# A chunked delta rule and a PReLU layer on one core: weight fetches issued one by one between the stages, and one step's squares moved

## The chip, the core and the metric

The kernel runs on one core of a Trainium2 chip. A core has four compute engines with instruction queues of their own: TensorE (PE, matrix products, with its weight loads shown as PEld), VectorE (DVE), ScalarE (ACT) and GpSimd (POOL). SyncE (SP) only issues DMAs here. The engines meet through semaphores. The metric is the device time of one execution in microseconds (us); lower is better.

## What is computed

Two blocks follow each other. The first is a delta-rule attention with batch 4, 8 heads, 768 tokens and head size 48; the second is a feed-forward layer on the 3072 tokens of width 384, with 2048 hidden units and a PReLU with one slope per unit.

```python
for t in range(S):
    y[:, :, t] = q[:, :, t] @ state
    v_old = state.T @ kt                     # kt: the key of t, divided by its norm
    state = state + beta_t * outer(kt, v[:, :, t] - v_old)
x = y as (tokens, heads * head size)         # 3072 x 384
h = x @ w_in                                 # 384 x 2048
g = max(h, 0) + alpha * min(h, 0)
out = g @ w_out                              # 2048 x 384
```

All is float32.

## The kernel before

**Tiling.** The 768 tokens are cut into 12 chunks of 64. A *step* is one chunk of two batch rows, so there are 24 steps, numbered from 0. A step needs its keys, values and queries, the squares of its keys (for the norms), the products of its keys with each other, the inverse of a triangular matrix made from these, a product with the carried state, its outputs, and the next state. Two steps of one chunk give 256 rows for the feed-forward layer. The first layer (`ffn_in`, products on L1068) has 16 column blocks of 128, each the sum of three products; after two column blocks, a relu on ScalarE (L1078) and two slope operations on VectorE (L1080) empty the PSUM bank. Two banks (`p_ffn`) take turns. The second layer of the first two chunks is `ffn_out` (L1111).

**Weights.** Both weight matrices are loaded once and rounded into another form on the chip. `w_in` is loaded in 12 pieces of 512 KB (piece 1 to 12; three pieces serve four column blocks), `w_out` in 16 pieces of 384 KB. A piece is fetched by one DMA from SP into a staging space (L216) and then converted by two ScalarE operations (L233, L235), one of VectorE (L249) and one of POOL or VectorE (L256). The staging spaces are borrowed: pieces 1 to 6 of `w_in` land where `w_out` will be, the others in `space_out`, `more`, `sums` and `turned`; the pieces of `w_out` use three slots of `space_out` and free parts of `w_out`. A fetch call `fetch(n)` issues all pieces up to the n-th that have not been issued. The converting generator also issues fetches when a piece is done: for `w_in` all the rest after the first piece (argument `limit` 0, L1654), for `w_out` one further piece per converted piece, if its staging space is free.

**Order.** The order of the instructions on each engine is the order in which the program's Python emits them; nothing reorders them. The engines then run their queues in order, each instruction waiting for its semaphores. SP too issues its DMAs in order: a DMA that waits holds all that are queued behind it. DMAs from SP use eight completion semaphores in turn, so a DMA also waits until the one eight places ahead has landed.

**The stages around the change.** After a prologue, `first_chunk` (from L1572) finishes steps 0 and 1; within it the q loads of steps 2 and 3 are issued (L1604), with `fetch_in(11)` behind them (L1605). `second_pair` (from L1763) does steps 2 and 3 and mixes in the first layer of chunk 0: the calls `alongside(p, c)` emit p matmuls of that layer and c conversion half-steps. `keys(k)` in it flips the keys of step k, squares them on ScalarE (L379), sums the squares on VectorE (L386) and issues the load of the keys three steps later. `fetch_out(4)` stands in it at L1813. A `weave` follows in which the first layer of chunk 1 (`ffn_in(1)`) runs beside the rest of the `w_out` conversion, beside `statics` (from L1620: squares, norms and key products of steps 8 and on) and beside `eliminate`, the triangular inverse on VectorE (L558, L564). `squares(n)` is the ScalarE square and the VectorE sum for step n; `weigh(n)` takes the root (L401, L402) and the reciprocal.

Of the kernel before, what the change touches and what calls it, by code (L numbers as in the profile page):

```python
# [43 lines left out]
def kernel(  # L44
# [105 lines left out]
    def load_q(n):  # L150
        if n < N:
            fetch(q, n, q_pad[n % NQ][:, :, 0:D])
# [36 lines left out]
    def weights(pieces, stages, ids, done, limit=None, pool=0, pace=None):  # L189

        count = len(pieces)
        fetched, begun = [], []  # L200

        def words(i):
            w = stages[ids[i]]
            dst, src = pieces[i]
            shape = list(dst.shape)
            n = shape[1] * (shape[2] if len(shape) > 2 else 1)
            w = w[:, 0 : 2 * n]
            if len(shape) > 2:
                return w.rearrange("p (f e) -> p f e", f=shape[1]), n
            return w, n  # L210

        def fetch(n):
            while len(fetched) < min(n, count):
                i = len(fetched)
                assert ids[i] not in ids[len(done) : i]
                nc.sync.dma_start(out=words(i)[0], in_=pieces[i][1].bitcast(U32))  # L216
                fetched.append(i)

        def flat(x):
            return x.rearrange("p f d -> p (f d)") if len(x.shape) > 2 else x  # L220

        def halves(i):
            w = flat(words(i)[0]).rearrange("p (e w) -> p e w", w=2)
            return w[:, :, 0], w[:, :, 1], flat(pieces[i][0])

        def begin_half(n):

            while len(begun) < min(n, 2 * count):
                i = len(begun) // 2
                assert i < len(fetched)  # L230
                lo, hi, dst = halves(i)
                if len(begun) % 2 == 0:
                    nc.scalar.activation(dst.bitcast(U32), lo, ACT.Copy, scale=2.0**-29)  # L233
                else:
                    nc.scalar.activation(  # L235
                        lo.bitcast(FP32), hi.bitcast(FP32), ACT.Prelu,
                        scale=2.0**-112, alpha=-(2.0**32),
                    )
                begun.append(i)

        def begin(n=None):
            begin_half(len(begun) + 1 if n is None else 2 * n)

        def finish():
            for i in range(count):
                n = 2 * min(i + 2, ahead[0])
                begin_half(max(n - 1, 2 * (i + 1)))
                lo, _, dst = halves(i)
                nc.vector.tensor_scalar(  # L249
                    out=lo, in0=lo, scalar1=3, scalar2=None, op0=ALU.logical_shift_left  # L250
                )
                yield

                begin_half(n)
                engine = nc.gpsimd if i < pool else nc.vector
                engine.tensor_tensor(  # L256
                    out=dst.bitcast(U32), in0=lo, in1=dst.bitcast(U32), op=ALU.add
                )
                done.append(i)
                n = len(fetched)  # L260
                last = min(count, limit or count, n + pace if pace else count)
                while n < last and ids[n] not in ids[i + 1 : n]:
                    n += 1
                    fetch(n)
                yield

        return fetch, begin, finish()
# [240 lines left out]
    NJ = 4  # L508
# [912 lines left out]
    in_done, out_done = [], []  # L1421
# [150 lines left out]
    def first_chunk(convert, mask):  # L1572

        both = (0, 1)
        ahead[0] = 0
        for n in both:
            place_small(n)

        def own(n):
            return own_values(n, ps_big()[:, :, 0:WY])  # L1580

        def rounds(i):
            for x in [one_round(n, i, ps_big()[:, :, 0:WY]) for n in both]:
                now(x)

        now(matrix(0, ps_big()[:, :, 0 : G * C]))
        turn_matrix(0, nc.scalar)
        scale_first(1, nc.vector)
        z_0 = own(0)
        now(z_0)  # L1590
        turn_values(0, nc.gpsimd)
        convert(1)
        now(matrix(1, ps_big()[:, :, 0 : G * C]))
        z_1 = own(1)
        now(z_1)
        turn_values(1, nc.scalar)
        turn_matrix(1, nc.scalar)
        convert(2)
        begin_in(4)
        for n in both:  # L1600
            mask(n)
        nc.gpsimd.memset(q_pad[0][0:1, 0, 0:1], 0.0)
        for i in both:
            load_q(i + 2)  # L1604
        fetch_in(11)  # L1605
        for i in range(3):
            rounds(i)
        y_0 = outputs(0, ps_big()[:, :, 0:WY])
        now(y_0)
        convert(2)  # L1610
        now(outputs(1, ps_big()[:, :, 0:WY]))
        to_ffn(0, ps_ffn())
        to_ffn(1, ps_ffn())
        convert(1)
        for n in range(2, NJ):
            place_small(n)
        begin_in()
        ahead[0] = FT * DM

    def statics(first, last):  # L1620
        if first > 0:
            squares(first)
        for n in range(first, last + 1):
            if n < last:
                squares(n + 1)
            now(weigh(n))
            flips(n, N)
            yield
            if n > 0:
                load_early(n + NKE)  # L1630
            if n > first:
                now(grams(n - 1))
            yield
        now(grams(last))
        yield
# [15 lines left out]
    stages += [sums.rearrange("p i s e -> p (i s e)").bitcast(U32)[:, 2 * n : 3 * n]]  # L1651
    stages += [rest.bitcast(U32)]
    ids = [*range(len(pieces))]
    fetch_in, begin_in, conv_in = weights(pieces, stages, ids, in_done, 0, len(pieces))  # L1654
    PARTS_IN = 2 * len(pieces)

    pieces = [(w_out[:, f], moe_w_out[f * 128 : (f + 1) * 128]) for f in range(FT)]
# [101 lines left out]
    def alongside(products, pieces, *gens):  # L1759
        gens = [(part(first_in, products), products), (part(convert_on, pieces), pieces), *gens]  # L1760
        weave(*[x for x in gens if x[1] > 0])

    def second_pair():  # L1763

        n, m, x = 2, 3, NJ
        both = (n, m)

        def burst(step, width):
            p = ps_big()
            pieces = []  # L1770
            for i in range(2):
                pieces += step(n + i, p[:, :, i * width : (i + 1) * width])
            now(pieces)

        def keys(k):
            flip_more(k)
            squared(k)
            norms(k)
            load_early(k + NKE)

        def through(i, p):
            now(through_state(i, None, p))

        now(next_state(0))
        load_late(2)
        for i in both:
            scale_first(i)
        alongside(2, 2)
        now(next_state(1))
        load_late(3)  # L1790
        keys(x)
        alongside(3, 3)
        burst(matrix, G * C)
        for i in both:
            turn_matrix(i, nc.gpsimd)
        now(weigh(x))
        alongside(3, 2)
        for i in both:
            flips(N, i)
            load_q(i + 2)  # L1800
        alongside(2, 1)
        keys(x + 1)
        alongside(2, 1)
        y = ps_big()
        through(n, y[:, :, 0 : G * D])
        alongside(2, 1)
        through(m, y[:, :, G * D : 2 * G * D])
        now(weigh(x + 1))
        alongside(3, 2)
        burst(own_values, G * D)  # L1810
        for i in both:
            turn_values(i, nc.gpsimd)
        fetch_out(4)  # L1813
        alongside(3, 2)
        now(grams(x))
        alongside(2, 2)
        burst(lambda i, p: one_round(i, 0, p), G * D)
        load_v(4)
        alongside(2, 1)
        keys(x + 2)  # L1820
        alongside(2, 2)
        burst(lambda i, p: one_round(i, 1, p), G * D)
        now(weigh(x + 2))
        alongside(2, 1)
        now(grams(x + 1))
        alongside(2, 1)
        burst(lambda i, p: one_round(i, 2, p), G * D)
        alongside(2, 1)
        keys(x + 3)
        alongside(2, 1)  # L1830
        now(grams(x + 2))
        now(weigh(x + 3))
        alongside(2, 1)
        burst(outputs, G * D)
        alongside(3, 2)
        now(grams(x + 3))
        alongside(2, 1)
        for i in both:
            to_ffn(i)
        alongside(2, 1, (part(blocks, 5), 5))  # L1840
        for i in both:
            now(next_state(i))
            load_late(i + 2)
            load_v(i + 3)
            alongside(2, 0, (part(blocks, 1), 1))
        alongside(IN_PARTS - 45, 0, (part(blocks, 1), 1))
# [174 lines left out]
```

## Time and profile before

| | us |
|---|---|
| median of 3 runs (656.79 to 661.25) | 657.06 |
| the profiled execution | 656.12 |
| its span, from first to last instruction | 654.3 |
| PE busy / VectorE / ScalarE / POOL | 634.4 / 481.5 / 258.4 / 122.5 |

The profile is of one execution, and all durations below come from it; 1.8 us lie outside its span. "L1068" is line 1068 of the kernel before. A row of the timeline is: start, duration, engine, line, operation, output <- inputs, and in brackets how long the engine stood idle before it and what ended that. "Granted clock" is the share of full speed that the throttle lets TensorE have; "DMA share" is the mean busy share of the 16 DMA engines, and can exceed 1 a little in short stretches.

### The profile page before, as it was taken

Reading aid. Unit: us, or ns where it says so; the run is one execution under the profiler, and the core shown is the slowest. Engines: PE = TensorE matmul, PEld = TensorE weight load, DVE = VectorE, ACT = ScalarE, POOL = GpSimd, SP = SyncE. Lnnn points to the kernel's source line nnn. Section 1 sums busy time; section 2 is a strip of 40 time slices with the busy share of each in tenths; the row PEclk is TensorE's granted clock in tenths of the full one; section 3 lists DMA queues with packets and bytes.
Section 4 is the critical chain, followed back from the end, with each engine's and each line's share of the span. In section 5 each row is a group of like instructions: output and inputs, shape, how many; then the busy total and the mean of one; then the engine's idle time right before and its main releaser. Section 6 shows DMA issues by size and latency. Waiting matters only on the chain.

```text
span 654.3 us, 21366 instructions
## 1 busy us (share of the span) xinstructions
PE 634.4 (97%) x9157; PEld 560.6 (86%) x9157; DVE 481.5 (74%) x1155; ACT 258.4 (39%) x605; POOL 122.5 (19%) x243
## 2 busy tenths in 40 slices
PE   6979999999999999999999999999999999999997
PEld 4657878566789988989988988988989999999997
DVE  5846789768999788578769658769868668477383
ACT  6637655245445244144244143133145145042140
POOL 6257511010001000010000010000044043062250
PEclk9979999999999999999999999999999999999999
DMA  8876454112422222121121111121121210100000
GB/s 159 231 205 167 144 115 134 36 39 50 76 44 45 42 47 38 37 51 38 35 43 26 30 41 32 28 45 29 33 43 27 50 27 2 35 5 2 24 1 25
DMA packets 108974, 37.27 MB, mean 57 GB/s; under 512 B 102048, under 2 KB 105264, under 8 KB 108880
## 3 DMA queue, kind: packets, MB, share of 16 engines
q1 hardware_dynamic: 107008, 35.42, 24.7%
q8 instruction: 72, 1.18, 0.7%
q10 hardware_dynamic: 1872, 0.49, 0.4%
q14 instruction: 22, 0.18, 0.1%
HBM read 31.17 MB, written 4.72 MB: 55 GB/s over the span
## 4 chain that ended last, share of the span: by engine, by line
PE 86%; DVE 6%; ACT 3%; issue 2%; DMA 2%; SPq 1%; POOL 0%; ACTq 0%
PE p_ffn L1068 23%; PE p_ffn L1133 17%; PE p_more L1385 8%; PE p_more L1301 5%; PE p_ffn L1111 4%; PE p_ffn L1291 3%; PE p_ffn L1385 3%; PE p_ffn L1296 2%; PE p_pair L423 2%; PE p_pair L800 2%; PE p_pair L923 2%; PE p_pair L740 2%; PE p_pair L910 2%; PE p_pair L479 2%; PE p_pair L788 1%
## 5 line engine op out<-in xcount | busy, mean ns | idle before, releaser
L1068 PE MATMUL p_ffn<-xt,w_in 128*128 128x256 f32 x768 | 178.6, 385 | 1.9 <-DVE sums L1080 1.2
L1068 PEld LDWEIGHTS p_ffn<-xt,w_in 128*128 128x128 f32 x768 | 142.2, 191 | 22.7 <-issue 2.0
L1078 ACT ACTIVATE act<-p_ffn 128x512 f32<-128x512 f32 x56 | 33.4, 597 | 82.2 <-PE p_ffn L1068 82.0
L1080 DVE SCALAR_TENSOR_TENSOR act<-act,al_t,p_ffn 128x256 f32<-128x256 f32 x112 | 48.6, 476 | 22.8 <-ACT act L1078 22.6
L1325 POOL TENSOR_TENSOR k_t<-k_t 128x128 f32<-128x128 f32 (+1 forms) x48 | 29.5, 615 | 167.5 <-ACT k_t L1320 165.0
L564 DVE TENSOR_TENSOR block<-block,prod 128x30 f32<-128x30 f32 (+9 forms) x150 | 49.9, 333 | 5.1
L558 DVE TENSOR_TENSOR prod<-block 128x30 f32<-128x30 f32 (+9 forms) x150 | 49.2, 328 | 3.6 <-POOL block L548 2.3
L412 POOL TENSOR_TENSOR beta_t<-beta_t,rec 128x8 f32<-128x8 f32 x20 | 5.2, 258 | 237.3 <-DVE rec L406 227.7
L1133 PE MATMUL p_ffn<-w_out,act 128*128 128x192 f32 x288 | 49.6, 328 | 0.0
L966 ACT COPY xt<-p_pair 128x384 f32<-128x384 f32 x22 | 10.4, 479 | 93.1 <-PE p_pair L962 79.3
L1133 PEld LDWEIGHTS p_ffn<-w_out,act 128*128 128x128 f32 x288 | 46.6, 190 | 0.3
L1325 POOL TENSOR_TENSOR block<-block 128x128 f32<-128x128 f32 (+1 forms) x48 | 27.6, 575 | 16.7 <-ACT block L1320 14.2
L1291 PE MATMUL p_ffn<-xt,w_in 128*128 128x256 f32 x96 | 28.7, 381 | 0.5 <-DVE o_sb L1153 0.5
L752 ACT COPY inv<-p_pair 32x256 f32<-32x256 f32 x40 | 14.5, 362 | 24.9 <-DVE u L914 24.1
L1339 DVE SCALAR_TENSOR_TENSOR act<-block,al_t,act 128x256 f32<-128x256 f32 x32 | 19.7, 657 | 5.2 <-ACT block L1335 5.1
L1153 DVE TENSOR_TENSOR o_sb<-u,p_ffn 128x192 f32<-128x192 f32 x24 | 8.0, 352 | 20.8 <-PE p_ffn L1133 20.0
L923 PEld LDWEIGHTS p_pair<-u,a_t 64*64 64x64 f32 x768 | 13.9, 137 | 10.5 <-issue 8.4
L792 ACT COPY y<-p_pair 128x384 f32<-128x384 f32 x22 | 10.6, 481 | 30.8 <-PE p_pair L788 29.2
L818 DVE TENSOR_TENSOR r<-v_raw,p_pair 64x192 f32<-64x192 f32 (+1 forms) x60 | 21.2, 353 | 1.0
L1385 PE MATMUL p_more<-w_out,act 128*128 128x192 f32 x128 | 21.9, 329 | 0.0
L1320 ACT COPY k_t<-p_more 128x512 f32<-128x512 f32 x16 | 9.4, 586 | 31.4 <-PE p_more L1301 26.7
L800 PE MATMUL p_pair<-beside,k_t 48*64 48x112 f32 x704 | 21.4, 259 | 0.2 <-ACT beside L451 0.2
(280 smaller groups left out, 1412.8 us busy)
## 6 DMA issues: line engine op xcount, KB each, us to landing
v_raw<-in_v_dram SPq DMA_DIRECT2D x48, 96.0 KB, 2.9
qp<-in_q_dram SPq DMA_DIRECT2D x48, 96.0 KB, 3.0
out_dram<-o_sb SPq DMA_DIRECT2D x90, 48.0 KB, 1.6
kl<-in_k_dram SPq DMA_DIRECT2D x88, 48.0 KB, 2.5
space_out<-in_moe_w_out_dram SPq DMA_DIRECT2D x11, 384.0 KB, 4.0
ke<-in_k_dram SPq DMA_DIRECT2D x43, 96.0 KB, 3.0
w_out<-in_moe_w_in_dram SPq DMA_DIRECT2D x6, 512.0 KB, 7.2
w_out<-in_moe_w_out_dram SPq DMA_DIRECT2D x5, 384.0 KB, 4.7
```

Of the source, the lines that this page charges most:

```text
L558: nc.vector.tensor_tensor(out=prod, in0=r[:, 0:j, j : j + 1].to_broadcast([128, j, n]), in1=r[:, j : j + 1, j + 1 : HB].to_broadcast([128, ...
L564: nc.vector.tensor_tensor(out=r[:, 0:j, j + 1 : HB], in0=r[:, 0:j, j + 1 : HB], in1=prod, op=ALU.add)
L800: nc.tensor.matmul(p[half(t ^ a), a, g], k_t[n][dims(a), g, half(t)], beside[bp][dims(a), t, g])
L923: nc.tensor.matmul(p[half(t), a, g], a_t[n][half(t ^ a), a * G + g], us[n][half(t ^ a), a, g])
L1068: nc.tensor.matmul(p_h[:, i], w_in[:, t, (f + i) * 128 : (f + i + 1) * 128], xt[:, t], start=(t == 0), stop=(t == KT - 1),)
L1078: nc.scalar.activation(g, p_h, ACT.Relu, scale=-1.0)
L1080: nc.vector.scalar_tensor_tensor(out=g[:, i], in0=g[:, i], scalar=al_t[:, f + i : f + i + 1], in1=p_h[:, i], op0=ALU.mult, op1=ALU.add,)
L1133: nc.tensor.matmul(p, x(i), w(i), start=(i == 0), stop=(i == FP - 1))
L1291: nc.tensor.matmul(p[:, f * 256 : f * 256 + 256], w(2, f), xt[:, 2], start=True, stop=False)
L1301: nc.tensor.matmul(q[:, j], a, b, start=True, stop=True)
L1325: nc.gpsimd.tensor_tensor(out=dst, in0=a, in1=b, op=ALU.add)
L1385: nc.tensor.matmul(p, x(i), w(i), start=(i == 0), stop=(i == FP - 1))
```

## The change

Three edits. First, the conversion of `w_in` no longer issues the remaining fetches when its first piece is done (`limit` 6 in place of 0), and `fetch_in(11)`, which stood behind the q loads, becomes `fetch_in(8)`; pieces 9 to 12 are issued one at a time in `second_pair`. Second, `fetch_out(4)` becomes four calls, of which the last three stand behind the v load of step 4 and behind two of the `keys`. Third, the squares of step 8 are emitted at the end of `second_pair`, behind `to_ffn`, and no longer at the start of `statics`.

```diff
@@ first_chunk
         for i in both:
             load_q(i + 2)
-        fetch_in(11)
+        fetch_in(8)
@@ statics
-        if first > 0:
+        if first > 2 * NJ:
             squares(first)
@@ the pieces of w_in
-    fetch_in, begin_in, conv_in = weights(pieces, stages, ids, in_done, 0, len(pieces))
+    fetch_in, begin_in, conv_in = weights(pieces, stages, ids, in_done, 6, len(pieces))
@@ second_pair
         now(next_state(0))
         load_late(2)
+        fetch_in(9)
...
         now(next_state(1))
         load_late(3)
+        fetch_in(10)
         keys(x)
...
         for i in both:
             flips(N, i)
             load_q(i + 2)
+        fetch_in(11)
         alongside(2, 1)
         keys(x + 1)
+        fetch_in(12)
...
             turn_values(i, nc.gpsimd)
-        fetch_out(4)
+        fetch_out(1)
...
         load_v(4)
+        fetch_out(2)
         alongside(2, 1)
         keys(x + 2)
+        fetch_out(3)
...
         keys(x + 3)
+        fetch_out(4)
...
         for i in both:
             to_ffn(i)
+        squares(x + 4)
         alongside(2, 1, (part(blocks, 5), 5))
```

On SP this gives the order: q loads, pieces 7 and 8, four k_late loads, piece 9, four k_late loads, piece 10, a k and four q loads, piece 11, a k load, piece 12, the first piece of `w_out`, a v load, the second, a k load, the third to fifth, a k load, the sixth to eighth, and behind eight k_late and four v loads the ninth and tenth.

## The prediction

> **What bounds the kernel now.** I read the page first (busy time, slices, queues), then the waits of TensorE (PE), then the chain of work that ended last, in order of time. From the page:
>
> ```profile
> PE 634.4 (97%) x9157; PEld 560.6 (86%) x9157; DVE 481.5 (74%) x1155; ACT 258.4 (39%) x605; POOL 122.5 (19%) x243
> ...
> PEclk9979999999999999999999999999999999999999
> ...
> q8 instruction: 72, 1.18, 0.7%
> ```
>
> PE is busy for 97% of the span, so time can be won only where PE stands idle or runs slowly: the third slice (33 to 49 us) is the one dip of the granted clock after the start. The waits of PE (total us, times, longest) beyond the first input loads:
>
> ```profile
> PE p_pair L923 <- issue: 4.3, 1, 4.3
> PE p_ffn L1068 <- DVE sums L1080: 1.2, 1, 1.2
> PE p_pair L850 <- issue: 1.1, 1, 1.1
> ```
>
> Two of the three are "issue": nothing that the profile shows was awaited. The chain (start, us, what) around the larger one, and two stretches (busy time of PE, PEld, DVE, ACT, POOL, then granted clock, DMA share, GB/s):
>
> ```profile
> 35.20 0.28 PE p_pair L923 x3
> 35.48 4.28 issue
> 39.76 1.10 PE p_pair L923 x29
> 40.86 1.56 PE p_ffn L962 x6
> 42.42 1.04 PE p_pair L939 x32
> 43.46 1.55 PE p_ffn L1068 x4
> 45.01 0.61 PE p_pair L939 x32
> ```
> ```profile
> 35.00:40.00 5.00, 0.52 (x11) 0.43 (x15) 0.64 (x2) 0.48 (x1) 4.28 (x8) 0.76 0.99 365
> 40.00:45.00 5.00, 5.00 (x75) 3.75 (x73) 2.65 (x5) 2.19 (x4) 0.74 (x2) 0.56 0.89 134
> ```
>
> PE stops in the middle of a group of 32 equal matmuls while the DMA engines are at 0.99; then it works at about half clock until 45 us. What does it await? The instruction queue moved 1.18 MB in 72 packets, 16 KB each, and 2 x 9157 PE instructions over 72 packets is 254 to a packet, or 127 matmuls with their weight loads. PE had done 600 matmuls when it stopped at 35.48, and 509 more when it stopped at 63.78 us: 4.0 packets. So I take both pauses for PE out of instructions, its next packet standing behind weights: six pieces of 512 KB are issued from 29.1 to 33.9 us, four of 384 KB from 55.9 to 58.7 us. Counting 127 matmuls back, the late packets could be asked for at 31.7 and 59.0 us, so they took 8.1 and 5.9 us; the packet begun at 31.7 had come within 3.0 us of 28.7, before the pieces moved (102 to 154 GB/s there).
>
> [...]
>
> **a. The first pause.** SyncE (SP) issues its DMAs in order. Before, the six late w_in pieces (7 to 12) went out ahead of four q loads; after, the q loads go at 34.12 us (as before, held by POOL's memset at 33.99) and take 0.65 us each, and only pieces 7 and 8 follow, near 36.8. Between 31.7 and 35.3 us no weights are in flight, so the packet should be there: 4.28 us go. With the pause goes the slow clock. The chain from 39.76 to 45.01 is 5.25 us; at full clock the same work is 0.49 (29 of L923, from 64 in 1.08 at 76.55), 0.82 (six L962, at 80.65), 0.62 (L939) and 1.06 us (four L1068), 2.99 in all, and 0.25 appears: the second three transposes wait for VectorE's copy of y (0.56), covered only by the first three (0.41), plus a hop. Saved 2.0, in all **-6.3 us**. Bounds: -6.6 (nothing appears) and -5.0 (1.3 us of pause left). From 45 to 63 us the chain is PE without a gap, so the gain is passed on.
>
> [...]
>
> What is late next? Each piece must land before ScalarE (ACT) converts it, for ACT is in order. With SP at 0.65 us per small load and 0.45 per piece, and ACT's rows (48.46, 54.36, 57.76, 60.69, 61.99) earlier by 6.3, pieces 7, 9, 10, 11 and 12 are issued near 36.8, 40.9, 44.0, 48.3 and 50.0 and wanted at 42.2, 48.1, 51.5, 54.4 and 55.7: 5.4 to 7.5 us each. Weight DMAs landed in 3.0 to 11.0 us, median 5.4, the longest being the last of six in a row; alone I take 4. Cost 0; a late piece 12 falls into ACT's idle 2.96 us before 66.34, and PE wants pieces 10 to 12 only at 77.56.
>
> **b. The second pause.** At the old 55.9 to 58.7 four w_out pieces went out; now one goes, then the v load, then a second. The packet wanted at 64.9 is asked for with about two pieces ahead instead of four: **-1.1 us**, bounds -0.3 and -1.15.
>
> **c. Later w_out pieces, and the squares.** Old times. (The fourth fetch call finds four pieces fetched already; fetching stays one piece behind.) *Piece 3* now stands behind the k load that waits until 67.86, is issued at 69.2, not 57.8, and is wanted by ACT at 70.08. Landing in 3.6 us, as piece 10 did (92.03 to 95.63), it holds ACT for 2.7 us; relu (71.46) and its slopes on VectorE slip, and the u sums end near 75.7, not 73.9. PE wants them at 76.48: nothing lost, 0.8 us left. *Piece 6* goes at 76.65 behind the next k load and is wanted at 78.15, but ACT's next work waits for PE until 81.17: free up to a landing of 4.0. *Piece 9* is different. It was issued near 77.5; now it comes behind eight k_late and four v loads, where piece 10 was, at 92.03. The old rows of ACT there:
>
> ```profile
> 93.16 0.55 ACT L233 ACTIVATE w_out<-space_out 128x384 uint32<-128x384 uint32 x1
> 93.62 0.57 ACT L1078 ACTIVATE sums<-p_ffn 128x512 f32<-128x512 f32 x1
> ...
> 95.63 0.56 ACT L233 ACTIVATE w_out<-space_out 128x384 uint32<-128x384 uint32 x1 [0.98 <-DMA space_out<-in_moe_w_out_dram]
> ```
>
> The first becomes piece 9, landing at 95.6; the relu behind it frees a PSUM bank for PE's group at 96.34. Step by step: 95.6 + 0.46 (convert) + 0.60 (relu) + 0.87 (two slopes) + 0.14 = 97.7, so that group starts 1.35 us later than before.
>
> The squares of step 8 leave this stretch: ACT's square (0.47) and VectorE's sum (0.5) run near 82 us, where they push the slopes back by 0.4. In return ACT's L401 at 90.31 no longer waits for a sum made at 89.73, the relu of 91.59 can run two us sooner, and PE's wait of 1.15 us at 92.09 shrinks to about 0.15. But the next group waits for piece 9 anyway, so this gain is lost inside the 1.35. Together **+1.3 us**; bounds -0.2 (landing in 3.0, and SP 0.9 us sooner: one k_late load took 1.51 us there, not 0.60) and +2.0 (VectorE, 98% busy from 100 to 110, stays behind and delays one more group).
>
> **Sum.** -6.3 - 1.1 + 1.3 = -6.1 on the profiled execution's 656.12 us: 650.0. The median of the runs shown, 657.06, lies 0.94 above that execution, so **650.9**; own range 649.1 (-6.6 - 1.15 - 0.2) to 653.8 (-5.0 - 0.3 + 2.0), both with the 0.94. One per cent, about what a measurement can tell from no change here, is 6.6 us: the forecast sits just inside it.
>
> **Rivals.**
> *A, the pauses are no fetch* (0.08). Then 4.28, 2.0 and 1.1 stay and only c acts: 656.12 + 1.3 + 0.94 = 658.4. For it: the profile names no releaser. Against: the counts, and DMA at 0.99 beside the one pause, full at 61 to 63 us before the other.
> *B, slower: late w_out pieces in ACT's order* (0.05). If pieces 3, 6 and 9 land in L us instead of 3.6, PE loses (L - 4.4) + (L - 4.0) + (L - 2.3), against 7.4 won: it turns slower at L = 6.0. At 9.1, as the piece into sums took, it loses 16.6: 666.3. For it: six of the moved pieces took 6 to 11 us. Against: those stood in one burst; w_out pieces took 4.0 and 4.7 us (medians), and between 65 and 69 us the DMA engines are all but idle.
> *C, the packets are late elsewhere* (0.13). From 34 to 53 us loads and pieces now follow each other closely, and a packet wanted near 52 or 57 us may wait. [...]
>
> **Chances.** The forecast 0.74, A 0.08, B 0.05, C 0.13. The range 649.0 to 655.0 takes in the forecast's bounds and C, and leaves out A, B and 0.05 of tails. Faster by over 1% (below 650.5) is nearly half of the forecast's share and a tail of it where c costs nothing: 0.40. Slower by over 1% is B from L = 8.2 on: 0.04. Within 1%: 0.56.
>
> **What would show it.** Right: no "issue" wait of over 0.5 us on PE, granted clock 1.00 from 35 to 45 us, L939's second group at 45.01 now near 38.7; ACT waiting for a DMA at its third and ninth w_out piece; PE waiting for DVE L1080 once, for about 2 us, at the old 95 to 98, and no more at 92. Wrong: pauses that stay in place (A), or turn up at another multiple of 127 matmuls (C); ACT waits of over 5 us for DMAs before 82 (B).

## The result and the profile after

The changed kernel takes 653.44 us (median of 20 runs, 652.05 to 657.0) against 656.91 us of the kernel before (20 runs, 654.94 to 661.25): a ratio of 0.9946, 95% interval 0.9932 to 0.9961. It is faster by half a per cent, 3.5 us. The forecast was 650.9; the measured time lies inside the range, on the same side, and the gain is a little over half of what was expected. The profiled execution after took 652.51 us with a span of 650.7 us, 3.6 us less than the span before.

From the page after (busy time per engine; the granted clock in 40 slices):

```profile
PE 633.7 (97%) x9157; PEld 559.3 (86%) x9157; DVE 481.9 (74%) x1155; ACT 257.9 (40%) x605; POOL 124.0 (19%) x243
...
PEclk9999999999999999999999999999999999999999
```

The dip of the clock in the third slice is gone, and the work of the engines is what it was. The chain of work that ended last, around the place of the old pause (start, us, what):

```profile
34.41 0.28 PE p_pair L923 x3
34.69 0.44 issue
35.13 0.70 PE p_pair L923 x29
35.83 0.02 issue
35.85 0.57 DVE y L866
...
38.71 0.61 PE p_pair L939 x32
```

The pause has shrunk from 4.28 to 0.44 us, the 29 matmuls of L923 behind it take 0.70 us in place of 1.10, and the wait of the transposes for VectorE's copy of y (L866) has appeared, as the working said. The same stretches as before in the kernel after (busy time of PE, PEld, DVE, ACT, POOL, then granted clock, DMA share, GB/s), with five microseconds ahead of them:

```profile
30.00:35.00 5.00, 4.27 (x195) 3.66 (x195) 4.16 (x8) 3.85 (x8) 4.96 (x5) 1.00 0.02 5
35.00:40.00 5.00, 4.68 (x109) 3.68 (x110) 4.18 (x7) 2.27 (x5) 4.41 (x6) 1.00 0.69 129
40.00:45.00 5.00, 5.00 (x87) 4.26 (x86) 2.85 (x6) 4.94 (x11) 4.26 (x7) 1.00 1.05 293
```

The DMA engines stand idle (0.02) while the packet of instructions that PE wants at 34.7 us can be fetched, and the granted clock stays at 1.00. What was lost again shows in the waits of PE in the kernel after (total us, times, longest), of which these are the ones near the change:

```profile
PE p_ffn L1068 <- DVE prod L558: 2.4, 1, 2.4
PE p_pair L923 <- DVE u L905: 1.4, 2, 1.2
PE p_pair L850 <- issue: 0.7, 1, 0.7
...
PE p_ffn L1068 <- DVE sums L1080: 0.5, 1, 0.5
PE p_pair L923 <- issue: 0.4, 1, 0.4
```

and in ScalarE's timeline (start, duration, engine, line, operation, in brackets the idle time before it and what ended that):

```profile
56.35 0.69 ACT L233 ACTIVATE w_in<-sums 128x512 uint32<-128x512 uint32 x1 [1.88 <-DMA sums<-in_moe_w_in_dram]
59.65 0.68 ACT L233 ACTIVATE w_in<-turned 128x512 uint32<-128x512 uint32 x1 [1.89 <-DMA turned<-in_moe_w_in_dram]
...
68.10 0.57 ACT L233 ACTIVATE w_out<-space_out 128x384 uint32<-128x384 uint32 x1 [3.35 <-DMA space_out<-in_moe_w_out_dram]
...
77.30 0.56 ACT L233 ACTIVATE w_out<-w_out 128x384 uint32<-128x384 uint32 x1 [3.41 <-DMA w_out<-in_moe_w_out_dram]
...
90.45 0.55 ACT L233 ACTIVATE w_out<-space_out 128x384 uint32<-128x384 uint32 x1 [4.90 <-DMA space_out<-in_moe_w_out_dram]
```

ScalarE waits for pieces 11 and 12 of `w_in` and for pieces 3, 6 and 9 of `w_out`; before, it waited for one piece in all, 0.98 us. Of the signs that the prediction named, three came: the clock, the second group of L939 near 38.7 us, and the waits for pieces 3 and 9. Three went another way: an "issue" wait of 0.71 us is left, piece 6 is awaited too, and PE's one wait of about 2 us (2.38) stands at 86.2 us, two groups of products ahead of where it was forecast. The further "issue" waits of rival C have not come: PE has only those of 0.7 and 0.4 us. Laying the same PE instruction of both profiles side by side shows where PE's lead was won and lost:

| PE instruction | before | after | lead |
|---|---|---|---|
| second group of L923, start | 35.20 | 34.41 | 0.79 |
| L423 behind the second L939 | 45.55 | 39.26 | 6.29 |
| L850 behind the second pause | 64.93 | 58.18 | 6.75 |
| L923 of steps 2 and 3 | 76.48 | 71.04 | 5.44 |
| third group of `ffn_in(1)`'s later half, behind L423 | 96.34 | 92.54 | 3.80 |
| first L1111 | 112.25 | 108.52 | 3.73 |

The first 0.79 us come from ahead of that group. 0.51 of them are a short stop that the kernel before makes at 31.9 us (more of it below) and the kernel after does not; the rest lies in the prologue, where PE's waits for the key loads add up to 5.2 us before and 4.6 after (4.4 to 5.4 in the profiles of this case). In the profiles below, the second group of L923 starts between 34.4 and 37.1 us in kernels that are the same up to there. For the rest I therefore use the stretch from that group to the first L1111: 77.05 us before, 74.11 after. The short stop lies outside it.

### The profile page after: what moved, and what is told of

The parts are those of the page before. It is cut to its first block, busy times and chain, and to the rows that moved or that the text cites. A ratio compares the mean times of both kernels' runs of the same rounds, so it can differ in the third digit from the quotient of the medians.

```text
span 650.7 us, 21360 instructions
## 1 busy us (share of the span) xinstructions
PE 633.7 (97%) x9157; PEld 559.3 (86%) x9157; DVE 481.9 (74%) x1155; ACT 257.9 (40%) x605; POOL 124.0 (19%) x243
## 4 chain that ended last, share of the span: by engine, by line
PE 81%; DVE 6%; DMA 3%; SPq 2%; ACT 2%; issue 1%; POOL 0%; ACTq 0%
PE p_ffn L1068 21%; PE p_ffn L1133 17%; PE p_more L1385 8%; PE p_more L1301 5%; PE p_ffn L1111 4%; PE p_ffn L1291 3%; PE p_ffn L1385 3%; PE p_ffn L1296 2%; PE p_pair L423 2%; PE p_pair L800 2%; PE p_pair L923 2%; PE p_pair L740 2%; PE p_pair L910 2%; PE p_pair L939 1%; DMA space_out<-in_moe_w_out_dram 1%; PE p_pair L479 1%
## 5 line engine op out<-in xcount | busy, mean ns | idle before, releaser
L966 ACT COPY xt<-p_pair 128x384 f32<-128x384 f32 x22 | 10.4, 478 | 90.7 <-PE p_pair L962 76.9
L1111 PE MATMUL p_ffn<-w_out,act 128*128 128x384 f32 x64 | 21.7, 490 | 0.0
```

The source lines that it names most:

```text
L1111: nc.tensor.matmul(p_o[u], gs[f // 2][:, f % 2, u * 128 : (u + 1) * 128], w_out[:, f], start=(f == 0), stop=(f == FT - 1),)
```

## The experiments

Theory T is the prediction's: the first pause is PE out of instructions behind a burst of weights, and what is lost later comes from late `w_out` pieces. Rival W puts that loss on the late pieces 11 and 12 of `w_in`; rival S on the moved squares; rival A says the pauses are no instruction fetch.

**Is the pause an instruction fetch?** The kernel before, with 32 more small matmuls in the prologue:

```diff
-    short(5, ps_one())
+    short(37, ps_one())
```

> The kernel before with 32 more matmuls of 32x32 in the prologue (about 0.7 us of PE), their result unused. If the first pause is PE out of instructions at a packet's border, PE stops 32 matmuls earlier in the program: not behind the third of the 32 matmuls of the second group of L923, but with some 3 left in the group of 32 before it (the first L923, its last three), again after about 600 recorded matmuls from the start, and for 3 to 5 us. The second pause moves 32 matmuls earlier too. If the pause belongs to an instruction or to a hidden wait at that place of the program (rival A), it stays behind the third matmul of the second group, now after about 632.

Its PE timeline, and PE's counts (the x behind the second number) up to the two pauses:

```profile
32.07 0.32 PE L850 MATMUL p_pair<-act 64*64 64x48 f32 x4 [0.34 <-DVE act L888]
35.40 2.49 PE L850 MATMUL p_pair<-act 64*64 64x48 f32 x92 [3.02 <-issue]
37.67 1.34 PE L850 MATMUL p_pair<-r,act 64*64 64x48 f32 x36
40.50 0.99 PE L850 MATMUL p_pair<-r,act 64*64 64x48 f32 x26 [1.49 <-issue]
```
```profile
0.00:35.30 35.30, 26.72 (x473) 20.06 (x473) 22.53 (x74) 21.89 (x56) 15.96 (x54) 1.00 0.88 219
...
0.00:39.50 39.50, 30.34 (x601) 23.49 (x601) 24.75 (x78) 22.04 (x56) 17.80 (x56) 0.96 0.90 234
```

PE stops after 473 and after 601 records. In the kernel before it had stood after 473 (0.51 us, put down to ScalarE's L235) and after 600 (4.28 us):

```profile
32.42 0.61 PE L850 MATMUL p_pair<-act 64*64 64x48 f32 x26 [0.51 <-ACT w_out L235]
```
```profile
0.00:31.70 31.70, 24.74 (x473) 17.81 (x473) 23.08 (x76) 20.32 (x54) 14.09 (x53) 1.00 0.85 190
...
0.00:36.00 36.00, 27.61 (x600) 20.21 (x600) 25.80 (x80) 22.70 (x57) 18.03 (x57) 1.00 0.86 202
```

The places in the program have moved by 64 records: the first stop came 68 records into the run of L850 on `act`, now 4; the second three records into the second group of L923, now in the L850 ahead. So the 32 added matmuls stand in the trace as 64 records, two for each; my "32 earlier" left that out. The counts stay and the instructions differ: the stop belongs to a border in the instruction stream, not to an instruction. The two stops together cost 4.8 us in the one and 4.5 in the other; which of the two borders is hit harder differs. The expected 3 to 5 us did not come at the second border (1.49), and the second pause of the kernel before, expected 32 matmuls earlier, did not come at all. This is one execution.

The kept traces hold more: the start and length of each packet of the instruction queue. They settle it.

| stop of PE, and where | packet moves, us | PE goes on | behind the packet's end |
|---|---|---|---|
| before, 473 records | 29.75 to 30.81 | 32.42 | 1.61 |
| before, 600 | 37.44 to 38.33 | 39.76 | 1.43 |
| before, second pause | 62.70 to 63.68 | 64.93 | 1.25 |
| shifted, 473 | 33.02 to 33.98 | 35.40 | 1.42 |
| shifted, 601 | 37.91 to 38.86 | 40.50 | 1.64 |
| after, 600 | 32.78 to 33.80 | 35.13 | 1.33 |
| after, second pause | 55.26 to 56.71 | 58.18 | 1.47 |

After every stop PE goes on 1.25 to 1.64 us behind the end of a packet. The packet behind the large pause began to move 5.0 us after PE had passed the border ahead (32.42 us), with the DMA engines at a share of 0.92 in between; in the kernel after, with the DMA engines idle (0.06), 1.1 us after it (31.63 us). Once begun, it took 0.9 and 1.0 us. So PE waits for its instructions, and the packet stands behind the weights before it moves: rival A falls.

**Which edit wins, which loses?** `w_in` spread alone (the `w_out` edits and the squares undone), and `w_in` spread with the squares moved:

```diff
-        fetch_out(1)
+        fetch_out(4)
...
-        fetch_out(2)
...
-        fetch_out(3)
...
-        fetch_out(4)
```

> Only the w_in fetches are spread; the w_out fetch call of four pieces and the squares are as before. Theory T (the first pause and its slow clock are worth 6.3 us, and what is lost later comes from the late w_out pieces 3, 6 and 9): 6.3 us faster than before, near 650.6; no wait of PE for VectorE's u at the outputs of steps 2 and 3, PE's wait of about 1.15 us for the slopes near the old 92 us stays, no ACT wait of over 1.5 us for a w_out piece. Rival W (the loss comes from pieces 11 and 12 of w_in, which hold ACT for 1.9 us twice, and this runs on): PE still waits 1.2 us for u, and the gain is 3.5 to 5 us only.

> The changed kernel with the w_out fetch call of four pieces put back: w_in spread and squares moved. Theory T: 6.3 plus about 1.0 for the squares, 7.3 us faster than before, near 649.6, and 3 to 4 us faster than the changed kernel. Rival W: no faster than the changed kernel, 3.5 to 4.5 us ahead of before.

The spread alone takes 651.74 us against 656.64 of before: 0.9914 (0.9882 to 0.9945); with the squares 650.83: 0.9891 (0.9844 to 0.9938). The first gain, 4.9 us, lies in W's range (3.5 to 5) as well as near T's 6.3; what tells them apart is PE's wait for u. Both kernels were timed again, beside the changed kernel.

> The changed kernel once more, as the measure for the three beside it: 3 to 4 us faster than before, with the waits of its first profile (PE for u about 1.2 us, one of about 2.4 us for the slopes after the transposes).

> w_in spread and squares moved, w_out fetched four at once, timed again beside the changed kernel. Theory T (late w_out pieces 3, 6 and 9 cost the changed kernel about 3 us, less the 0.5 of the second pause): 2 to 3.5 us faster than the changed kernel, no PE wait over 0.6 us between 40 and 105 us. Rival W (late pieces 11 and 12 of w_in): within 1 us of the changed kernel.

> w_in spread alone, again. If the squares are worth what PE's wait at the old 92 us shows (1.15 us, less 0.5 that is left in the kernel with both): 0.6 to 1.2 us slower than with the squares moved. If they are worth nothing (rival S): the same within 0.3 us, or faster.

| kernel | median, us | ratio to before | 95% interval | L923 to L1111, us |
|---|---|---|---|---|
| before | 657.01 | 1 | | 77.05 |
| as changed | 654.55 | 0.9965 | 0.9945 to 0.9985 | 74.11 and 74.40 |
| `w_in` spread alone | 650.85 | 0.9908 | 0.9889 to 0.9927 | 71.38 and 71.27 |
| `w_in` spread, squares moved | 650.80 | 0.9902 | 0.9885 to 0.9919 | 70.02 and 70.62 |

The intervals of the last two do not meet that of the changed kernel: without the spread of `w_out` the kernel is some 3.7 us faster (654.55 - 650.80), and faster than both kernels of this change. The changed kernel gained 2.5 us here, where 3 to 4 were expected, with the expected waits. Rival W falls as the sole cause: with `w_in` spread alone, ScalarE waits for pieces 11 and 12 as it does in the changed kernel, and PE does not wait for u (VectorE's L905, from which the outputs of steps 2 and 3 are made). ScalarE's waits for DMAs in that kernel, and PE's only wait of over 0.5 us from 40 to 105 us:

```profile
56.22 0.68 ACT L233 ACTIVATE w_in<-sums 128x512 uint32<-128x512 uint32 x1 [1.21 <-DMA sums<-in_moe_w_in_dram]
60.02 0.67 ACT L233 ACTIVATE w_in<-turned 128x512 uint32<-128x512 uint32 x1 [2.40 <-DMA turned<-in_moe_w_in_dram]
88.87 0.56 ACT L233 ACTIVATE w_out<-space_out 128x384 uint32<-128x384 uint32 x1 [0.16 <-DMA space_out<-in_moe_w_out_dram]
```
```profile
87.31 2.83 PE L1068 MATMUL p_ffn<-xt,w_in 128*128 128x256 f32 x12 [1.14 <-DVE sums L1080]
```

The last line is the old wait at 92 us. In the kernel with the squares moved it is replaced by one of 0.50 us:

```profile
82.90 5.42 PE L1068 MATMUL p_ffn<-xt,w_in 128*128 128x256 f32 x24 [0.50 <-DVE act L1080]
```

The stretch is shorter by 0.65 to 1.36 us for it; the medians differ by 0.9 in one timing and by 0.05 in the other, where 0.6 to 1.2 was expected, so the squares' worth is seen in the trace but not settled in time.

**The other two edits alone.** The kernel before with only the `w_out` fetches spread, and with only the squares moved:

> The kernel before with only the w_out fetches spread. Theory T: pieces 3, 6 and 9 land late and cost 1 to 4 us, the second pause shrinks by 0.5: 0.5 to 3.5 us slower than before, the first pause of 4.3 us unchanged. If the late pieces cost nothing (rival W): 0.5 to 1.1 us faster than before, for the second pause alone.

> The kernel before with only the squares of step 8 moved. Theory T: PE's wait for the slopes at 92 us shrinks from 1.15 to about 0.15, 1.0 us faster. Rival S (the moved square delays the relu and the slopes near 82 us and nothing comes back): 0 to 0.5 us slower, the wait at 92 us as before or longer.

The first takes 656.49 us, 0.9988 (0.9961 to 1.0014); the second 655.73, 0.9986 (0.9959 to 1.0013), both on 656.64. Neither can be told from no change, and the figures of T and of S for the squares both lie inside the interval. For the spread of `w_out`, T had expected 0.5 to 3.5 us slower, and the interval reaches only to 0.9: most of T's range was missed, and the 0.5 to 1.1 us faster of rival W lies inside. In the first profile ScalarE waits for `w_out` pieces 3, 6 and 9 (2.70, 3.06 and 1.88 us), PE for VectorE's slopes 1.05, 1.14 and 0.74 us between 90 and 98 us, and not for u; the second pause is gone. So the late pieces cost here too, 1.8 us more of waits for slopes than before (2.93 against 1.15), and the 1.15 us of the second pause come back. The wait for u needs both spreads: it is there in the three profiles with `w_in` and `w_out` spread and piece 3 behind the key load (0.87 to 1.25 us), and not with either spread alone. The pauses at the two early borders are 3.40 and 1.96 us in this kernel, 1.52 and 2.21 us in that of the squares, so a single profile of these says little on sums.

**Which piece is late, and does it come from its place?** The changed kernel with the third and fourth `w_out` piece issued ahead of the load of keys that waits, and with the third alone:

```diff
+        fetch_out(4)
         keys(x + 2)
-        fetch_out(3)
...
         keys(x + 3)
-        fetch_out(4)
```
```diff
+        fetch_out(3)
         keys(x + 2)
-        fetch_out(3)
```

> The changed kernel with pieces 3 and 4 of w_out issued ahead of the load of the keys two stages on, so that they no longer stand behind a load that waits; all else is as changed. Theory T: piece 3 lands in time (no wait of PE for u, 1.25 us), fetching is again one piece further ahead, so pieces 6 and 9 are early too: 3 to 4 us faster than the changed kernel, 6.5 to 7.5 faster than before, near 650. Rival W (pieces 11 and 12 of w_in are what is late): as the changed kernel.

> The changed kernel with only the third w_out piece issued ahead of the load of keys it stands behind; the fetching of the later pieces stays one piece behind. Theory T splits the loss: the wait for u (1.2 us) goes, pieces 6 and 9 are late as before, so the 2.4 us wait after the transposes and ACT's wait for piece 9 stay: 0.8 to 1.6 us faster than the changed kernel, and 1 to 2.5 us slower than w_in spread with squares moved. If piece 3 carries the whole loss by holding the chain of key loads: as fast as w_in spread with squares moved.

The first takes 650.92 us, 0.9915 (0.9884 to 0.9946) on 656.64: as fast as the kernel that fetches four at once. Its stretch is 71.33 us, with a second pause of 0.90. ScalarE still waits there for pieces 11 and 12 of `w_in` (1.04 and 2.72 us), which speaks against rival W again. The second takes 654.69, 0.9962 (0.9943 to 0.9982) on 657.01, no faster than the changed kernel beside it (654.55). Its PE waits:

```profile
60.97 0.26 PE L850 MATMUL p_pair<-sums 64*64 64x48 f32 x2 [1.57 <-issue]
86.56 5.42 PE L1068 MATMUL p_ffn<-xt,w_in 128*128 128x256 f32 x24 [1.44 <-DVE prod L558]
94.52 4.12 PE L1068 MATMUL p_ffn<-xt,w_in 128*128 128x256 f32 x18 [2.11 <-DVE sums L1080]
```

The wait for u is gone, as expected of piece 3 in time. But ScalarE still waits 3.41 us for piece 6 and 5.61 for piece 9, and PE now waits longest behind piece 9 (2.11 instead of 0.47) and at the second pause (1.57). So the expected gain of 0.8 to 1.6 us did not come; time won ahead of piece 9 is handed back at piece 9. What matters is how many pieces the fetching is ahead: one piece more brings 650.9, one piece merely earlier brings nothing (the two intervals just meet, at 0.994).

The traces show which piece sets the end of the loss. From the start of the second L939 of steps 2 and 3 to the group behind L423 at which piece 9 counts, PE takes:

| kernel | us |
|---|---|
| before; `w_in` spread alone (two profiles) | 12.41; 12.39 and 12.38 |
| as changed (two profiles) | 14.05 and 14.11 |
| changed, third piece ahead | 14.60 |
| changed, squares back in `statics` (below) | 14.33 |
| `w_out` spread alone | 14.23 |
| changed, third and fourth piece ahead | 11.37 |
| `w_in` spread, squares moved (two profiles) | 11.39 and 11.35 |

With piece 9 behind the k_late and v loads it is 14.05 to 14.60, however long PE waited on the way. In the chain of the kernel after, PE's L939 frees the k_late loads, these and the v loads hold piece 9 until 86.45 us, it lands at 90.37, and its conversion, a relu and the slopes start PE at 92.54. So the waits ahead of that group, piece 6's among them, are not added to the loss: what they do not take, the wait for piece 9 takes.

**The squares in the changed kernel.** The changed kernel with the squares back in `statics`:

> The changed kernel with the squares of step 8 back in the later stage. Theory T: the moved squares hardly matter there, because PE's next group waits for piece 9 anyway; within 0.5 us of the changed kernel. Rival S (the square delays the first relu after the transposes by 0.5 us and the wait of 2.4 us grows by it): 0.4 to 1 us faster than the changed kernel. If the squares pay in full: 1.0 us slower than the changed kernel.

654.08 us, 0.9961 (0.9942 to 0.9979) on 656.64; the changed kernel has 0.9946 and 0.9965. No difference, as T had it, though the intervals reach some 1 us to each side and would hide the 0.4 to 1 us of the other two expectations. Its stretch is 74.82 us: PE waits 0.73 and 1.15 us for the slopes ahead, and 1.16 behind piece 9.

## Why the prediction was right, and where its sizes were off

The direction, the range and the mechanism of the first pause held; the loss behind it was sized at less than half. By steps, with the lead of the table:

**a, first pause: -6.3 forecast, -5.5 measured** (6.29 - 0.79). The pause gave 3.84 (4.28 to 0.44): the border still costs PE 0.44 to 0.72 us in the kernels with `w_in` spread, where the working had it at nothing. It had read the packet begun at 31.7 us as one that came in time; but PE had stopped 0.51 us for it, a wait that the profile puts down to ScalarE. The clock gave 1.66 (restart to L423: 5.79 to 4.13 us), where 2.0 was worked out from rows at full clock: the 29 matmuls of L923 take 0.70 us in the chain, not 0.49. That the slow clock goes with the pause was the author's reading of one dip; the runs agree: behind 0.44 us the clock stays at 1.00, and in the shifted program, which stops for 3.02 us until 35.40, its mean is 1.00 over the first 36.0 us and 0.94 over the first 40.4. How long a stop must be for it was not determined: in the kernel with only the squares moved, 32 matmuls of L850 take 1.11 us (0.68 before) shortly behind a stop of 1.52. The spread alone won 4.9 and 6.2 us in the two timings. The stops behind 473 and 600 recorded matmuls, each with its weight load, lie 127 apart, the length of a packet that the prediction worked out from 72 packets.

**b, second pause: -1.1 forecast, -0.46 in the profile after** (1.15 to 0.71, 6.75 - 6.29 = 0.46). This term was mis-sized, and the number of `w_out` pieces does not set it: with four pieces at once, in the kernels with `w_in` spread, the pause is 0 to 0.2; with `w_out` spread too it ranges from 0 to 1.57 (0 in the second profile of the changed kernel). The working left out that pieces 11 and 12 of `w_in` now go out at 51.5 and 53.6 us, around 52.7 us, where PE passes the border ahead. That they hold the packet up fits its start, 2.6 us after that border, against 3.7 before and 1.3 with `w_out` spread alone, but was not tested. How often the pause strikes was not determined, so its size here stays open.

**c, late pieces: +1.3 forecast, +3.0 measured** (6.75 - 3.73). This is the step that failed. *Piece 3* was to cost nothing with 0.8 us to spare; PE waited 1.25 us for u, and 1.31 us of the lead went there (6.75 - 5.44). It landed in 4.3 us (63.77 to 68.10), not 3.6, and it was issued 1.3 us later than reckoned (63.77 against 69.2 - 6.75 = 62.45). That lateness came from the pieces before it. SP was behind the plan: pieces 11 and 12 went out at 51.5 and 53.6 us instead of 48.3 and 50.0, and landed in 4.8 and 6.1 us. ScalarE's wait for them, costed at nothing because PE wanted their weights much later, held the square that releases the key load in front of piece 3. *Piece 6* was "free up to a landing of 4.0"; it took 5.5 us (71.84 to 77.30), with two key loads ahead of it and two further pieces behind it:

```profile
70.52 1.28 SPq L137 DMA_DIRECT2D ke<-in_k_dram  x2
71.84 1.11 SPq L216 DMA_DIRECT2D w_out<-in_moe_w_out_dram  x2
73.06 1.23 SPq L216 DMA_DIRECT2D space_out<-in_moe_w_out_dram  x1
```

The copies of the outputs (L966), the relu and the slopes behind it slipped by 2 us, and PE waited 2.38 us at 86.2, a wait that the prediction did not have. About 0.5 us of it, an estimate from the rows, is the squares, which now stand ahead of that relu (ScalarE's at 78.50 us) and of its slopes (VectorE's at 79.06). *Piece 9* behaved as foreseen (issued at 86.45 behind k_late and v loads, landed in 4.0 us, ScalarE 4.90 us idle). PE, already late, waited only 0.47 there, but the start of that group is what piece 9 sets: 1.64 us of the lead went up to it (5.44 - 3.80), where 1.35 was forecast. So the term that was put at nothing and cost 1.3 us is piece 3; piece 6's wait came unforeseen and is covered by piece 9's.

Rival B's formula, which was set up for a slowdown, gives the same total by luck: with landings of 4.3, 5.5 and 4.0 us it gives (4.3 - 4.4) + (5.5 - 4.0) + (4.0 - 2.3) = 3.1 us, but nothing for piece 3, which cost 1.3, and 1.5 for piece 6, which added nothing. The forecast put one landing time of 3.6 in for all three, taken from a row where a single piece was under way. B's mechanism acted, late pieces in ScalarE's order, short of the point from which it decides.

**The squares** give what was worked out where pieces are in time: the way to the group of piece 9 is 1.0 us shorter with them moved (12.39 to 11.39), though a wait of 0.5 us is left and not of 0.15. Behind late pieces hardly any of it is left (14.33 us with the squares back, 14.05 and 14.11 with them moved), as the working said.

**The sum** by measured terms is -5.5 - 0.5 + 3.0 = -3.0, and with the 0.8 us ahead of the stretch -3.8; the profiled executions differ by 3.6 us, the medians by 3.5. The measured time lies near the upper end of the forecast's own range because b and c erred to the same side. That it stayed inside is in part luck: c went 1.0 past its bound of +2.0, and a and b kept off their worst bounds.

## What to carry to other kernels

An "issue" wait in a stretch of small matmuls, beside saturated DMA engines (here 4.28 us at a DMA share of 0.99), may be PE waiting for its own instructions: count matmuls between such pauses, shift them with a few added ones, and look where the packets of the instruction queue stand. Spreading a burst of large transfers took the pause from 4.28 us to 0.44 here, but each transfer moved behind others in an in-order queue must be costed with the landing time under the load it will then meet (4.3 and 5.5 us for pieces 3 and 6 here, 3.6 forecast), and at the next engine that waits for it in order (ScalarE, 3.35 and 3.41 us idle), not only at the final user. Here one half of the change won 5 to 6 us, and another half, meant in the same way, gave over 3 of them back.

## What the runs showed that was not expected

A border in PE's instruction stream costs 0.44 us in the kernel after although the DMA engines moved next to nothing in the five microseconds ahead (share 0.02); in another execution of the same program it was 0.72. The packets give the reason: from passing one border (31.63 us) to going on at the next (35.13) it takes 1.1 us until the packet moves, 1.0 for the packet and 1.3 behind it, 3.5 in all, and PE was there in 3.06 us. So PE stopped a little at this border even with idle DMA engines. The same border's pause under the burst varied from 1.49 to 4.28 us between executions, while the sum of the two neighbouring borders varied less (4.8, 5.4, 4.5; 3.7 in the kernel with the squares moved, where the first is put down to ScalarE). A wait for instructions can also be put down to another engine: the 0.51 us "ACT w_out L235" in the kernel before sits at the same border, 473 records in, at which 3.02 us are put down to "issue" once the program is shifted; and PE goes on 1.61 us behind a packet, as at the other stops.
